# Turning x by block transposes and memory-to-memory copies instead of matrix-engine transposes, and dealing the freed PSUM banks anew

## The chip, the cores and the metric

The kernel runs on one core of a Trainium2 chip. The metric is the device time of one execution in microseconds (us). The kernel before takes 598.78 us, the median of three runs (597.99 to 598.87). Five engines work side by side, each strictly in the order of its own program: PE (matrix products, with its weight loads listed as PEld), DVE (vector), ACT (scalar functions), POOL (a second, slower vector engine) and SP, which here only issues transfers. An engine waits for another one through semaphores. Matrix products land in PSUM, a small memory of banks; everything else lies in the on-chip memory.

## The reference

Eight batches of 576 tokens. Attention with two kinds of narrow masks gives x (576 x 512 per batch), and a token and channel mixer follows:

```python
scores = scale * np.matmul(q, k.transpose(0, 1, 3, 2))
# masks: heads 0-3 a window of 32, heads 4-7 a window of 32 with dilation 4
attn = softmax(np.where(masks, scores, -1e9));  x = np.matmul(attn, v)   # heads side by side
theta = x @ w_theta
zr, zi = x * np.cos(theta), x * np.sin(theta)
y = w_tok_r @ zr + w_tok_i @ zi            # over tokens, per batch
u = x + y
out = u + np.maximum(u @ w_ch, 0.0)
```

So x is needed in two layouts. The attention leaves it with the 128 channels of a pair of heads on the partitions and tokens along the rows (call it x turned), and the products x cos(theta), x sin(theta) need tokens on the partitions.

## The kernel before

All large products are made in float32 quality from split operands: a value is a high part and a low part, and each product is three matmuls (high x high, high x low, low x high). The high part is a cast on ACT, the low part a subtraction on POOL.

One batch goes through these stages. **Scores** (`scores`, L438): for each of four pairs of heads PE makes the scores `s`, DVE adds the mask and takes the row maximum (nine mask instructions, L406), ACT takes nine exponentials (L501), DVE the sums and their reciprocals (L504, L505), POOL scales the rows (L507). **Turn** (`turn`, L511): DVE turns the probabilities by eight block transposes (L522) per pair. **pv** (L600): PE multiplies with v into bank `v`; ACT copies the result out as x turned (`x_evac`, L578), and `x_split` (L582) makes its high and low part. **theta** (L669): five blocks of tokens in the order STS = 4, 0, 1, 2, 3, block 4 being the last 64 tokens; twelve matmuls per full block (L682). **trig** (L722) of a block: ACT rounds theta/2pi to a whole number K (L746), DVE takes the remainder (L748), which frees the bank of theta, ACT takes the sine (L754) and, in `cosine` (L693), the absolute value and the cosine (L695, L697). `natural` (L713) has PE transpose x into a PSUM bank `xn` (four transposes per block, L718), and DVE multiplies `xn` by sine and cosine (L760 and L702; L767 for block 4). `zsplit` (L630) splits each product into the buffers `zh` and `zl` (ACT L641, POOL L643). Block st gives the buffers number st (cosine) and 4 + st (sine); block 4 gives number 8.

**Token units** (`token`, L790): eight units of 27 matmuls (L804) per batch, each over all nine z buffers in the order KORD = 0, 4, 1, 5, 2, 6, 3, 7, 8; DVE then adds the result to x (L782), ACT and POOL split that again (L785, L787). **Channel units** (`chan`, L821): eight units of twelve matmuls (L834) and one DVE instruction each (L813); they share two PSUM banks `m` with the token units.

`phase` (L841) sets the order for batch b and the next batch nb: the eight token units of b with the scores, turns and pv of nb between them, then five times theta, a channel unit and trig, then the three channel units left, and then the next phase begins with the scores of pair 2 and the first token unit. The opening (batch 0 and half of batch 1) is ordered by a planner with ranks (`Order`), since the weights arrive then. Above that, the framework that builds the program runs its own timed model of all engines and moves an instruction of DVE, ACT, POOL or SP when the model says that its input is late; only PE's instructions, and in the opening all that `pin` marks, keep the written order. The sine and the exponential need different tables in ACT; `table` keeps those instructions in written order, so all sines of a phase come before the exponentials of the next.

PSUM before: scores and theta share the two banks `s` with theta's own `t`; `xn` takes `x` and, in turn, the pv bank `v`.

## Time and profile before

| | |
|---|---|
| median of three runs | 598.78 us |
| the profiled execution's own time | 597.07 us |
| its span (first to last instruction) | 595.3 us |
| PE busy | 569.7 us, 96% |
| DVE, ACT, POOL busy | 361.6, 351.1, 222.4 us |
| transposes of x on PE (L718) | 160, 20 per batch |
| one batch in the middle | 211.01 to 279.69 us |

The span lies inside the execution's own time; 1.8 us are outside it. A batch is best read at three points: the end of the last token unit (251.06 us in the batch above), the end of the last channel unit (279.69 us), and the end of the first token unit after it (284.67 us). PE works through one list without a choice, so what it waits for at these points is what a batch costs.

### The profile page before, as it was taken

The page shows a single profiled execution, that of the slowest core. Times are in us where ns is not written, and L with a number is a line of the kernel's source. Part 1 is how long each engine was busy: PE and PEld are TensorE (multiplying, and loading weights), DVE is VectorE, ACT ScalarE, POOL GpSimd, SP SyncE. Part 2 cuts the span into 40 slices and gives each one's busy share as a digit, 9 for nine tenths or more (in the row PEclk, how much of TensorE's full clock was granted, in tenths as well). Part 3 has the DMA queues.
Part 4 walks back from the last instruction along what each step waited for, and adds up shares of the span by engine and source line. Part 5 has one row for each costly group of instructions (what it writes and reads, how often), then busy time and mean ns, then how long its engine had stood idle before and what let it go on. Part 6 is the DMA issues. An engine that isn't in the chain of part 4 may idle for free.

```text
span 595.3 us, 14176 instructions
## 1 busy us (share of the span) xinstructions
PE 569.7 (96%) x5584; PEld 516.9 (87%) x5584; DVE 361.6 (61%) x1132; ACT 351.1 (59%) x939; POOL 222.4 (37%) x206
## 2 busy tenths in 40 slices
PE   5997898999999999999999999999999999999997
PEld 4744787979998899889998899989998899989997
DVE  3889888855765667465566567655665656445112
ACT  1498967687535955568553974468564785266110
POOL 2229854534322532326142442316324253315220
PEclk9999599999999999999999999999999999999999
DMA  8982347404650074302641054401742023001002
GB/s 303 398 339 61 121 160 246 142 1 141 182 160 3 2 241 142 101 2 89 197 139 62 1 181 151 154 1 40 231 142 73 0 81 100 1 1 53 28 1 81
DMA packets 26866, 67.76 MB, mean 114 GB/s; under 512 B 2992, under 2 KB 3248, under 8 KB 26800
## 3 DMA queue, kind: packets, MB, share of 16 engines
q1 hardware_dynamic: 26800, 66.86, 32.9%
q8 instruction: 44, 0.72, 0.5%
q14 instruction: 22, 0.18, 0.1%
HBM read 57.41 MB, written 9.44 MB: 112 GB/s over the span
## 4 chain that ended last, share of the span: by engine, by line
PE 49%; DVE 22%; ACT 21%; issue 3%; POOL 2%; DMA 2%; SPq 0%; ACTq 0%; DVEq 0%; POOLq 0%
PE y L804 27%; DVE pt L522 9%; PE c L834 8%; PE s L465 5%; ACT P L501 5%; PE o L614 4%; PE th L682 3%; ACT K L697 3%; ACT zh L641 3%; ACT g L754 2%; ACT K L695 2%; DVE P L406 2%; DVE K L702 2%; POOL P L507 2%; ACT L754 1%
## 5 line engine op out<-in xcount | busy, mean ns | idle before, releaser
L787 POOL TENSOR_TENSOR u<-x,u 128x288 fp32r<-128x288 f32 x64 | 54.9, 858 | 184.9 <-ACT u L785 162.2
L522 DVE STREAM_TRANSPOSE pt<-P 32x288 f32<-32x288 f32 x224 | 105.1, 469 | 21.1 <-POOL P L507 18.0
L834 PE MATMUL c<-u,late_wc 128*128 128x288 f32 x768 | 111.7, 296 | 0.8 <-DVE x L813 0.5
L834 PEld LDWEIGHTS c<-u,late_wc 128*128 128x128 f32 x768 | 106.2, 188 | 4.8 <-DVE x L813 2.0
L785 ACT CAST u<-x 128x288 fp32r<-128x288 f32 x64 | 27.5, 430 | 129.3 <-DVE x L782 129.3
L804 PE MATMUL y<-wtkh,zh 128*128 128x288 f32 x288 | 90.6, 315 | 1.1 <-ACT zh L641 1.1
L804 PE MATMUL y<-wtkh,zl 128*128 128x288 f32 x288 | 86.6, 301 | 3.7 <-POOL zl L643 3.7
L804 PE MATMUL y<-wtkl,zh 128*128 128x288 f32 x288 | 86.2, 299 | 0.0
L643 POOL TENSOR_TENSOR zl<-g,zh 128x512 fp32r<-128x512 f32 x40 | 52.6, 1316 | 79.1 <-ACT zh L641 66.7
L501 ACT ACTIVATE P<-P,mx 128x64 f32<-128x64 f32 x216 | 72.1, 336 | 16.8 <-DVE mx L495 16.8
L682 PE MATMUL th<-wthh,xh 128*128 128x512 f32 x224 | 76.3, 402 | 0.0
L782 DVE TENSOR_TENSOR x<-y,x 128x288 f32<-128x288 f32 x64 | 28.7, 450 | 66.8 <-PE y L804 64.0
L804 PE MATMUL y<-late_wt_b,zh 128*128 128x288 f32 x320 | 68.1, 297 | 0.0
L804 PE MATMUL y<-late_wt_a,zh 128*128 128x288 f32 x256 | 58.0, 308 | 2.7 <-DVE x L782 2.7
L804 PEld LDWEIGHTS y<-wtkh,zh 128*128 128x128 f32 x288 | 55.4, 192 | 4.8 <-ACT zh L641 2.3
L804 PEld LDWEIGHTS y<-wtkh,zl 128*128 128x128 f32 x288 | 55.3, 192 | 4.5 <-POOL zl L643 4.5
L804 PEld LDWEIGHTS y<-wtkl,zh 128*128 128x128 f32 x288 | 55.5, 193 | 0.3 <-issue 0.3
L643 POOL TENSOR_TENSOR zl<-K,zh 128x512 fp32r<-128x512 f32 x32 | 42.0, 1312 | 36.1 <-ACT zh L641 36.1
L507 POOL TENSOR_TENSOR P<-P,sm 128x576 f32<-128x576 f32 x32 | 37.5, 1172 | 43.8 <-ACT xh L590 19.3
L804 PEld LDWEIGHTS y<-late_wt_b,zh 128*128 128x128 f32 x320 | 51.4, 189 | 0.3
L682 PEld LDWEIGHTS th<-wthh,xh 128*128 128x128 f32 x224 | 42.1, 188 | 8.3
L804 PE MATMUL y<-late_wt_b,zl 128*128 128x288 f32 x160 | 47.3, 296 | 0.0
(103 smaller groups left out, 1110.0 us busy)
## 6 DMA issues: line engine op xcount, KB each, us to landing
q<-in_qT_dram SPq DMA_DIRECT2D x32, 576.0 KB, 4.2
va<-in_vw_dram SPq DMA_DIRECT2D x30, 320.0 KB, 3.2
out_dram<-x SPq DMA_DIRECT2D x32, 288.0 KB, 2.1
k<-in_kT_dram SPq DMA_DIRECT2D x28, 304.0 KB, 4.6
vb<-in_vw_dram SPq DMA_DIRECT2D x29, 256.0 KB, 3.4
st_wtk<-in_wtk_dram SPq DMA_DIRECT2D x8, 576.0 KB, 8.8
st_wth<-in_wth_dram SPq DMA_DIRECT2D x4, 512.0 KB, 9.8
st_wch<-in_wch_dram SPq DMA_DIRECT2D x4, 512.0 KB, 4.9
```

Source lines behind the costliest of these rows:

```text
L465: pe(nc.tensor.matmul(ps[64 * e:64 * e + 64, n - g0], q[:, qb], k[:, QB * qb:QB * qb + BW], start=not masked, stop=not masked or n == g1 - 1))
L501: table(nc.scalar.activation(P[:, n], P[:, n], AF.Exp, bias=mx[:, n:n + 1], scale=SCALE, accum_out=sm[:, n:n + 1]))
L507: pin(nc.gpsimd.tensor_tensor(P, P, sm.unsqueeze(2).to_broadcast([128, NJ, BW]), op=ALU.mult))
L522: pin(nc.vector.transpose(pmats[b, pr][k0:k0 + QB, :, hh, QB * e:QB * e + QB], P[p0:p0 + QB, :, QB * o:QB * o + QB]))
L614: pe(nc.tensor.matmul(ps[64 * hh:64 * hh + 64, BW * j:BW * j + BW], v[:, 64 * hh:64 * hh + 64], pmats[b, pr][:, j, hh], start=True, stop=T ...
L643: pin(nc.gpsimd.tensor_tensor(lo, z, hi.bitcast(F32), op=ALU.subtract))
L682: pe(nc.tensor.matmul(pt, l, r, start=(n == 0), stop=(n == 3 * NC - 1)))
L782: pin(nc.vector.tensor_tensor(x[:, ts], ps, x[:, ts], op=ALU.add))
L785: pin(nc.scalar.copy(uh[b, d][:, ts], x[:, ts]))
L787: pin(nc.gpsimd.tensor_tensor(ul[b, d][:, ts], x[:, ts], uh[b, d][:, ts].bitcast(F32), op=ALU.subtract))
L804: pe(nc.tensor.matmul(ps, l[:, cs], r, start=(n == 0), stop=(n == 3 * NK - 1)))
L834: pe(nc.tensor.matmul(ps, l[:, cs], r[:, ts], start=(n == 0), stop=(n == 3 * NC - 1)))
```

## The change

From batch 1 on PE no longer transposes x. `x_turn` has DVE transpose x turned in blocks of 32 x 32 into a buffer `xq`, one instruction of 128 x 576 per pair of heads. That puts each block right inside itself but leaves the blocks in the wrong place, and `x_move` puts them in place by copies within the on-chip memory: per block of 128 tokens 16 copies of 32 partitions x 128 values (16 KB), 8 for block 4, 72 per batch, all issued by SP. Their target `xn` is not a new buffer but the memory of the z buffers `zh4` to `zh8`, which hold the sine products of the previous batch until its last token unit has read them, and which take this batch's sine products afterwards. So the copies wait for the token units, and the split of the sine product now waits until both products of the block are made. DVE's products read `xn` from the on-chip memory (in a pattern of 16 runs of 32) instead of from PSUM. The theta blocks take the banks `t` and `x` in turn and leave the two banks `s` to the scores; `v` belongs to pv alone. The last hunk makes a descriptor scratch buffer smaller, which this kernel's transfers do not use.

```diff
-TP = {4: "t", 0: "s", 1: "s", 2: "t", 3: "s"}
-XP = {4: "x", 0: "v", 1: "x", 2: "v", 3: "x"}
+TP = {4: "t", 0: "x", 1: "t", 2: "x", 3: "t"}
...
             go(x_split(b, pr))
+            go(x_turn(b, pr))
...
-        pt, rel = yield from bank("t" if b == 1 else TP[st], f"th{b}_{st}")
+        pt, rel = yield from bank(TP[st], f"th{b}_{st}")
...
         yield None, ("xn", b, st)
-        px, rx = pxs[b, st]
         yield "DVE", dve(DM)
-        pin(nc.vector.tensor_tensor(z, px, f, op=ALU.mult))
+        by_x(b, st, z, f)
         signal(key)
         if kt is not None:
-            yield None, ("px", b, st)
-            give(*rx)
+            if not b:
+                yield None, ("px", b, st)
+                give(*pxs[b, st][1])
             yield from zsplit(b, kt, z, rel)
...
+    def x_turn(b, c):
+        yield None, ("xe", b, c)
+        if c == 0:
+            yield from take("xq", 1, b - 1)
+            xq[b] = cp.tile([128, 18, NC, QB], F32, tag="xq", name=f"xq{b}")
+        elif od.live:
+            yield None, ("got", "xq", b - 1)
+        yield "DVE", 1000
+        pin(nc.vector.transpose(xq[b][:, :, c], xf[b, c].rearrange("p (a s) -> p a s", s=QB)))
+        signal(("xq", b, c))
+
+    def x_move(b):
+        for c in range(NC):
+            yield None, ("xq", b, c)
+        if b == 1:
+            for d in range(NC):
+                yield None, ("tk", 0, d, 1)
+        for st in STS:
+            R = 64 if st == 4 else 128
+            kt = min(4 + st, 8)
+            xn = hp.tile([128, DM], F32R, tag=f"zh{kt}", name=f"xn{b}_{st}").bitcast(F32)
+            yield "DMA", dma(R // 128 * DM)
+            for a in range(R // QB):
+                for g in range(4):
+                    pin(nc.sync.dma_start(xn[QB * a:QB * a + QB, 128 * g:128 * g + 128],
+                                          xq[b][QB * g:QB * g + QB, 4 * st + a].rearrange("p a b -> p (a b)")))
+            xns[b, st] = xn[:R].rearrange("p (g c d) -> p c g d", g=4, c=NC)
+            signal(("xn", b, st))
+        give("xq", b - 1)
+
+    def rows(t):
+        return t.rearrange("p (c g d) -> p c g d", c=NC, g=4)
...
+    def by_x(b, st, z, f):
+        if b:
+            pin(nc.vector.tensor_tensor(rows(z), xns[b, st], rows(f), op=ALU.mult))
+        else:
+            pin(nc.vector.tensor_tensor(z, pxs[b, st][0], f, op=ALU.mult))
...
-            pin(nc.vector.tensor_tensor(g, px, g, op=ALU.mult))
+            by_x(b, st, g, g)
             signal(("px", b, st))
+            if b:
+                yield None, ("cos", b, st)
             yield from zsplit(b, 4 + st, g, rg)
...
         rest = UNITS[n:]
+        go(x_move(nb))
         for i, st in enumerate(STS):
             go(theta(nb, st))
...
+    go(x_move(1), 0)
     go(thetas(1), RANK["theta1"])
```

The order of the instructions that results moves at three places. In the rows below the names carry a block (or pair) and a serial number: `K_2` and `g_2` are the cosine and the sine of block 2, `c_3_1` a channel unit, `P_2` and `sm_2` the probabilities and sums of pair 2 of the next batch. Line numbers are each kernel's own: before L702/L760 are the products with x, L748 the remainder, L813 a channel unit's end, L406/L495 mask and maximum, L782 a token unit's end; in the changed kernel these are L764, L794, L860, L405/L494 and L829.

DVE before, at the end of a phase (blocks 1 to 3 of theta, the last channel units, then the next phase's masks):

```order
L702 TENSOR_TENSOR K_1_3365<-xn_1_3360,K_1_3365 128x512
L760 TENSOR_TENSOR g_1_3366<-xn_1_3360,g_1_3366 128x512
L748 SCALAR_TENSOR_TENSOR K_2_3414<-th_2_3382,K_2_3414 128x512
L813 SCALAR_TENSOR_TENSOR x_3_2173<-c_3_0_3395,x_3_2173 128x288
L702 TENSOR_TENSOR K_2_3414<-xn_2_3409,K_2_3414 128x512
L760 TENSOR_TENSOR g_2_3415<-xn_2_3409,g_2_3415 128x512
L748 SCALAR_TENSOR_TENSOR K_3_3464<-th_3_3431,K_3_3464 128x512
L813 SCALAR_TENSOR_TENSOR x_1_1963<-c_1_1_3481,x_1_1963 128x288
L702 TENSOR_TENSOR K_3_3464<-xn_3_3459,K_3_3464 128x512
L760 TENSOR_TENSOR g_3_3465<-xn_3_3459,g_3_3465 128x512
L813 SCALAR_TENSOR_TENSOR x_3_2173<-c_3_1_3511,x_3_2173 128x288
L406 ISA P_2_3526,mx_2_3527<-s_2_0_3529,mskb 128x64
```

DVE at the same place in the changed kernel:

```order
L860 SCALAR_TENSOR_TENSOR x_3_2234<-c_3_1_3682,x_3_2234 128x288
L764 TENSOR_TENSOR K_1_3546<-xn_1_3378,K_1_3546 128x512
L764 TENSOR_TENSOR g_1_3547<-xn_1_3378,g_1_3547 128x512
L405 ISA P_2_3697,mx_2_3698<-s_2_0_3700,mskb 128x64
...
L494 TENSOR_SCALAR mx_2_3698<-mx_2_3698 128x9
L794 SCALAR_TENSOR_TENSOR K_3_3635<-th_3_3607,K_3_3635 128x512
L503 TENSOR_SCALAR sm_2_3699<-sm_2_3699 128x9
L504 RECIPROCAL sm_2_3699<-sm_2_3699 128x9
L764 TENSOR_TENSOR K_2_3590<-xn_2_3395,K_2_3590 128x512
L764 TENSOR_TENSOR g_2_3591<-xn_2_3395,g_2_3591 128x512
L764 TENSOR_TENSOR K_3_3635<-xn_3_3412,K_3_3635 128x512
L764 TENSOR_TENSOR g_3_3636<-xn_3_3412,g_3_3636 128x512
```

Before, the products of blocks 1 to 3 stand among the channel units' ends and all of them ahead of the next masks. Now those of block 1 stand behind the last channel unit, block 3's remainder behind the masks, and the products of blocks 2 and 3 behind the sums of the exponentials of the next phase's first scores. This holds at the end of the phases that lead to batches 2 to 6. At the one that leads to batch 7, where no scores follow, the products of block 1 also stand behind the last channel unit, and block 3's remainder and the products of blocks 2 and 3 follow them at once.

POOL at the same place, before (L643 is the low part of a z buffer, L507 the scaling of `P_2`, L787 the low part of a token unit's sum):

```order
L643 TENSOR_TENSOR zl_5_3379<-g_1_3366,zh_5_3378 128x512
L643 TENSOR_TENSOR zl_2_3423<-K_2_3414,zh_2_3422 128x512
L643 TENSOR_TENSOR zl_6_3428<-g_2_3415,zh_6_3427 128x512
L643 TENSOR_TENSOR zl_3_3473<-K_3_3464,zh_3_3472 128x512
L643 TENSOR_TENSOR zl_7_3478<-g_3_3465,zh_7_3477 128x512
L787 TENSOR_TENSOR u_0_3603<-x_0_2726,u_0_3603 128x288
L507 TENSOR_TENSOR P_2_3526<-P_2_3526,sm_2_3528 128x576
```

and in the changed kernel (the scaling is L506):

```order
L643 TENSOR_TENSOR zl_5_3560<-g_1_3547,zh_5_3559 128x512
L506 TENSOR_TENSOR P_2_3697<-P_2_3697,sm_2_3699 128x576
L643 TENSOR_TENSOR zl_2_3599<-K_2_3590,zh_2_3598 128x512
L643 TENSOR_TENSOR zl_6_3604<-g_2_3591,zh_6_3603 128x512
L643 TENSOR_TENSOR zl_3_3644<-K_3_3635,zh_3_3643 128x512
L643 TENSOR_TENSOR zl_7_3649<-g_3_3636,zh_7_3648 128x512
L834 TENSOR_TENSOR u_0_3774<-x_0_2840,u_0_3774 128x288
```

The scaling of `P_2` has moved ahead of four low parts. ACT has the nine exponentials of `P_2` ahead of the casts zh_2, zh_6, zh_3 and zh_7 in the same way.

SP in the changed kernel, where the copies begin, with what each waits for (`DMAHW0` to `DMAHW7` are eight completion counters that the transfers take in turn):

```order
L219 DMA k_3_3274<-in_kT_dram 128x608
L742 DMA xn_0_3361<-xq_2869 32x128 [waits DVE_49,DMAHW6_49,PE_49,Pool_49]
L742 DMA xn_0_3361<-xq_2869 32x128
L742 DMA xn_0_3361<-xq_2869 32x128 [waits DMAHW0_49]
L742 DMA xn_0_3361<-xq_2869 32x128 [waits DMAHW1_49]
L742 DMA xn_4_3352<-xq_2869 32x128 [waits DMAHW2_49,PE_49]
L742 DMA xn_4_3352<-xq_2869 32x128 [waits DMAHW3_49]
```

All 72 copies stand between the last loads of k and v for a phase and the four stores of the batch's result. Each waits until the transfer eight places ahead of it has landed.

15 lines of the change are left out of this document (9 added, 6 removed).

## The prediction

> **What bounds the kernel now.** I read the page's first lines, then busy time by windows, then the chain of waits.
>
> ```profile
> span 595.3 us, 14176 instructions
> PE 569.7 (96%) x5584; PEld 516.9 (87%) x5584; DVE 361.6 (61%) x1132; ACT 351.1 (59%) x939; POOL 222.4 (37%) x206
> ```
>
> PE is the only engine near its limit; an average, so I look at one batch. The windows are 211.01 (scores of pair 2 begin) to 251.06 (last token unit ends), to 279.69 (last channel unit ends), to 284.71 (first token unit of the next phase ends); columns are PE, PEld, DVE, ACT, POOL busy, then clock and transfers.
>
> ```profile
> 211.01:251.06 40.05, 39.52 (x506) 37.85 (x506) 25.29 (x120) 21.19 (x83) 12.46 (x13) 1.00 0.51 166
> 251.06:279.69 28.63, 28.35 (x176) 25.20 (x176) 17.41 (x34) 21.01 (x39) 11.88 (x11) 1.00 0.06 21
> 279.69:284.71 5.02, 5.02 (x67) 4.79 (x67) 2.02 (x21) 4.13 (x18) 2.24 (x2) 1.00 0.84 285
> ```
>
> PE idles 0.8 us in 68.68: 211.01 to 279.69 is one batch, and each of the three stretches is as long as PE's work in it. The chain of waits shows the same, piece by piece:
>
> ```profile
> 276.23 3.46 PE c L834 x24
> 279.69 1.20 PE s L465 x36
> 280.89 3.78 PE y L804 x27
> ```
>
> The first token unit needs all nine z buffers and starts 1.2 us after the channel units. Before, it never waits for them. I call the ends of the last token unit, of the channel units and of the first token unit U, T and E: T - U = 28.63, E - T = 4.98, and E to the next U 35.1 us.
>
> **What leaves PE.** Twenty transposes per batch, in five groups. The timeline of PE (start, duration, engine, line) at block 4 of theta, a channel unit, a full block, another channel unit and a group:
>
> ```profile
> 251.06 0.39 PE L687 MATMUL th<-wthh,xh 128*128 128x512 f32 x1
> ...
> 252.90 1.74 PE L834 MATMUL c<-u,late_wc 128*128 128x288 f32 x12
> ...
> 254.84 0.48 PE L682 MATMUL th<-wthh,xh 128*128 128x512 f32 x1
> ...
> 257.66 1.74 PE L834 MATMUL c<-u,late_wc 128*128 128x288 f32 x12
> 259.24 0.60 PE L718 MATMUL xn<-idt,x 128*128 128x128 f32 x4
> 259.59 0.47 PE L682 MATMUL th<-wthh,xh 128*128 128x512 f32 x1
> ```
>
> A group holds PE 0.35 us from start to start (259.24 to 259.59), five groups 1.75. Block 4 of theta takes 1.84 (251.06 to 252.90), a full block 2.82 (254.84 to 257.66), a channel unit 1.58 (257.66 to 259.24): 1.84 + 4 x 2.82 + 8 x 1.58 = 25.8, which leaves 2.8 of T - U for the groups and about 1 us of waits for channel banks, which go too, since DVE's channel ends no longer stand behind products. I take -2.7 per batch, bounds -1.75 and -2.9. If nothing else happened, six batches like that and one in the opening would give -18.
>
> **What becomes late.** The diff does not show it, the order does: on DVE the products of blocks 2 and 3 now follow the sums of the next phase's exponentials. DVE works in order, so I walk from T along the engines with these durations (timelines of DVE, ACT and POOL at the end of this batch, and of ACT and DVE around the exponentials after the previous one):
>
> ```profile
> 278.60 0.68 DVE L760 TENSOR_TENSOR g<-xn,g 128x512 f32<-128x512 f32 x1
> 279.19 1.00 DVE L813 SCALAR_TENSOR_TENSOR x<-c,x 128x288 f32<-128x288 f32 x2
> 281.90 0.17 DVE L495 TENSOR_SCALAR mx<-mx 128x9 f32<-128x9 f32 x1
> 273.80 0.58 ACT L746 ACTIVATE K<-th 128x512 int32<-128x512 f32 x1
> 275.13 0.68 DVE L748 SCALAR_TENSOR_TENSOR K<-th,K 128x512 f32<-128x512 f32 x1
> 275.91 0.63 ACT L754 ACTIVATE g<-K 128x512 f32<-128x512 f32 x1
> 277.23 0.72 ACT L697 ACTIVATE K<-K,halfpi 128x512 f32<-128x512 f32 x1
> 278.71 0.62 ACT L641 CAST zh<-K 128x512 fp32r<-128x512 f32 x1 [0.76 <-DVE K L702]
> 279.95 1.28 ACT L501 ACT_TABLE_LOAD   x1
> 213.42 0.35 ACT L501 ACTIVATE P<-P,mx 128x64 f32<-128x64 f32 x1 [0.86 <-DVE mx L495]
> 216.56 0.18 DVE L504 TENSOR_SCALAR sm<-sm 128x9 f32<-128x9 f32 x1
> 216.77 0.22 DVE L505 RECIPROCAL sm<-sm 128x9 f32<-128x9 f32 x1
> 279.41 1.27 POOL L643 TENSOR_TENSOR zl<-K,zh 128x512 fp32r<-128x512 f32 x1 [1.52 <-ACT zh L641]
> 280.65 1.28 POOL L643 TENSOR_TENSOR zl<-g,zh 128x512 fp32r<-128x512 f32 x1
> ```
>
> The last channel end leaves DVE at T + 0.5 (279.19 + 1.00). Two products of 0.6 (from one start to the next, 278.60 to 279.19): T + 1.8. The first one's cast on ACT: T + 1.85; its low part on POOL, 1.28: T + 3.2. Only that frees the buffer in which ACT writes block 3's K (two such buffers go round): T + 3.8, the remainder on DVE 0.68: T + 4.55; the nine masks, which before were done by T + 2.2 (281.90), have ended by T + 3.5 behind the two products. Sine, absolute value, cosine on ACT run 2.05 us (275.91 to 277.95): T + 6.6. The table of the exponential 1.28: T + 7.9. Nine exponentials 3.1 (213.42 to 216.53): T + 11.05. Sum and reciprocal: T + 11.5. Now the four products, 2.4: the first at T + 12.2, the last at T + 14.0. POOL scales P_2 first (1.2 us as in the fence below, to T + 12.7) and then makes four low parts, one per 1.26: T + 17.9. PE needs the last of them for one matmul and then has three more of 0.13 (27 in 3.78 are 0.14 each): E = T + 18.4. Against T + 4.98 that is **+13.4** per batch. It replaces the slack that the products had among the channel units; what is late next is everything behind E, since PE has no other work there: the order has the token unit next. This walk without any further delay is the bound from below.
>
> **Products from memory beside POOL.** They read both inputs from memory now. Nearest row, the low part of x, also 128x512 from two inputs in memory:
>
> ```profile
> L596 DVE TENSOR_TENSOR xh<-x,xh x21: 677/686/1646, 101.1 to 509.8; 128x512 fp32r<-128x512 f32 x21
> 229.16 1.21 POOL L507 TENSOR_TENSOR P<-P,sm 128x576 f32<-128x576 f32 x1 [3.21 <-ACT xh L590]
> 229.28 1.65 DVE L596 TENSOR_TENSOR xh<-x,xh 128x512 fp32r<-128x512 f32 x1
> ```
>
> Alone it takes 0.686, as from PSUM. When POOL had started 0.12 us earlier, it ended at 230.93, 0.56 after POOL's end: it stood still until then. From T + 11.5 on POOL is never idle, so between 0 and 2.4 us (four products beside five POOL instructions, all in line) is added. I take **+1.9**, near the row in which both ran.
>
> The Trainium skill, "SBUF — State Buffer", section "Who interferes with whom", states that a DVE instruction with two on-chip inputs and a GpSimd instruction that reads the same memory exclude each other for their whole length. The trace agrees in the pair of rows above. By that rule the term would be the full 2.4 and the time some 3 us longer; by the median row it would be 0 and the time 10 us shorter.
>
> **The clock of PE.** PE waits for long only in the opening, and there a steady run of matmuls follows from 66.5 on:
>
> ```profile
> 66.00:71.00 5.00, 4.48 (x18) 4.48 (x19) 2.80 (x8) 5.00 (x27) 4.37 (x5) 0.50 0.01 3
> 71.00:76.00 5.00, 5.00 (x41) 4.92 (x41) 4.83 (x10) 4.86 (x9) 5.00 (x4) 0.96 0.00 0
> ```
>
> For about 4.7 us after work is steady again the granted clock stays at 0.50; of such 4.7 us about half is lost. I take **+2.1** behind each E and +0.4 for the last matmuls before it; bounds 0 and 3.
>
> **DVE's block transposes.** Four per batch, 128x576. Nearest row:
>
> ```profile
> L522 DVE STREAM_TRANSPOSE pt<-P 32x288 f32<-32x288 f32 x224 | 105.1, 469 | 21.1 <-POOL P L507 18.0
> ```
>
> If the time goes by elements in a row, 576 is 2 x 0.469 = 0.94; if by all elements, 8 x 0.469 = 3.75. A product of 128 partitions takes 0.68 / 512 = 1.3 ns per element of a row, this transpose of 32 partitions 0.469 / 288 = 1.6: the number of partitions hardly counts in these rows, so I take 0.9. They stand in front of the low parts of x and of the turns of P, where DVE is busy 25.29 of 40.05 us; a walk of that stretch like the one above finds one place that pinches, the end of the third token unit on DVE, at E + 17.6 behind a turn, whose bank PE wants at E + 17.2; in exchange the 0.5 us wait of that kind before the last unit goes. That is 0. At 3.75 each (15 per batch) DVE has 41 us for a 35 us stretch: +6 per batch.
>
> **The copies.** 72 per batch, on a queue where each waits for the one eight ahead.
>
> ```profile
> idb<-in_identb_dram SPq DMA_DIRECT2D x1, 32.0 KB, 1.7
> 237.69 0.33 SPq L231 DMA_DIRECT2D va<-in_vw_dram  x1
> ```
>
> Landing in 1.7 allows one per 0.21; issuing costs 0.33 for a load of 128 partitions. I take 0.3 each: they begin when zh4 has been read, U - 2.7, and the last lands near U + 21, before T. Needed are 24 at U + 15, 40 at T + 0.5, 56 at T + 11.5, 72 at T + 12.7 (T = U + 25.9). So they are hidden by the chain above; on their own they decide from 0.55 us per copy on. SP's queue behind them holds the result's stores, which wait for T + 0.5 anyway, and the loads of the next pair, used after E + 16: covered. That a product waits for eight counters instead of one I count as nothing beside these terms.
>
> **The banks.** theta block 1 takes the bank that block 4's remainder frees.
>
> ```profile
> 259.64 0.68 DVE L748 SCALAR_TENSOR_TENSOR K<-g,K 64x512 f32<-64x512 f32 x1 [0.33 <-ACT K L746]
> ```
>
> Before, that remainder ended at U + 9.3; block 1 could now start at U + 7.8 (1.84 + 1.58 + 2.82 + 1.58). Were DVE not earlier, PE would wait 1.5. But the turn of P_1 ahead of it on DVE waits for exponentials that hang on masks, and in my walk these come about 1 to 2 us earlier after E than before, since DVE has nothing else left to do there. I take 0, bounds 0 and +1.5.
>
> **Sum.** Per transition into batches 2 to 6: -2.7 + 13.4 + 1.9 + 0.4 + 2.1 = +15.1, times five = **+75.5**. Into batch 7 no scores follow, so the walk skips table, exponentials and P_2: K_3's remainder at T + 4.55, its cosine at T + 6.6, its products at T + 7.9, low parts to T + 12.4 (four from T + 7.3), E = T + 12.95. Before, from the chain of waits:
>
> ```profile
> 550.34 28.62 PE y L804 x216
> ```
>
> There (T = 550.34) E = T + 3.6 (an eighth of 28.62): +9.3, with 0.5 for POOL, 2.5 for the clock and -1.9 for PE's transposes **+10.4**. In the opening (batch 1; first row from the chain, second from DVE's timeline):
>
> ```profile
> 118.88 0.69 DVE g L743
> 141.26 0.69 DVE L702 TENSOR_TENSOR K<-xn,K 128x512 f32<-128x512 f32 x1
> ```
>
> The last block transpose stands just ahead of block 4's first instruction on DVE (118.88 before), so the copies start near 120 and end, at 0.3 each, near 144; the last product with x began at 141.26, so its low parts come some 5 us later while PE gains 1.8: **+4**, bounds -2 and +6. Together +90 on the profiled execution's 597.07: 687. The median is 1.7 above the profiled execution, so **688**.
>
> Its own range: with contention, clock and opening at their lower bounds (+10.7 x 5 + 7 - 2 = +59) 657; at the upper ones (block 1's bank, 2.4 and 3 for every batch, opening +6) about +110, 708.
>
> **Rivals.** (1) *PE's relief is all that counts*, the products come when PE wants them: 598.8 - 18 = 581. For it: PE at 96%. Against it: the order of DVE and ACT, which nothing at run time changes. 3%. (2) *The copies set the pace*: at 0.7 us each the last lands at U + 50, 11 later than the chain needs it, 67 more in six batches: 755. For it: many small copies in one queue; against it: 1.7 us for 32 KB with eight under way. 7%. (3) *The block transposes cost by all elements*: 6 x 6 more, 725. 8%. (4) *PE has room in the wait*, as if DVE's blocks overlapped better than my walk, half of the 13.4: 640 to 655. 5%. That x is still turned on PE is excluded by the order. My forecast has the remaining 77%.
>
> A measurement of this kernel tells 0.2% (1.2 us) from no change. Faster 3%, the same 1%, slower 96%. The range of 650 to 730 leaves out rivals 1 and 2, the lower part of 4 and the outer ends of 3.
>
> **What would show it.** Right: PE idle some 12 us behind T in batches 2 to 6, ended by zl (POOL) and zh (ACT); scaling of P_2 ahead of four low parts; PE's clock near 0.5 behind it; a batch of about 84 us; products of 0.69 alone and up to 1.9 beside POOL; copies landed before T. Wrong: DVE's products waiting on `xn` copies (rival 2), block transposes far above 1 us (rival 3), or a first token unit that ends before T + 15.

## The result and the profile after

The changed kernel takes 746.87 us, the median of four runs (744.9 to 747.51), against 598.83 us (597.99 to 598.95) for the kernel before: a ratio of 1.247, 95% interval 1.244 to 1.250. The prediction had the sign and missed the size: +148 where +90 was expected, and 746.9 lies outside the range of 650 to 730. The profiled execution took 744.9 us of which the span is 743.0.

The first lines of the page and its chain of waits by line (what each line of the program holds of the way to the end):

```profile
span 743.0 us, 14681 instructions
PE 591.1 (80%) x5444; PEld 522.6 (70%) x5444; DVE 388.4 (52%) x1160; ACT 352.9 (48%) x939; POOL 222.6 (30%) x206
PEclk9998999869999689995999859996799958997599
SPq L742 37%; PE y L851 17%; DVE pt L521 7%; ACT P L500 4%; PE o L613 3%; PE c L881 3%; POOL zl L643 2%; PE s L464 2%; DMA xn<-xq 2%; DVE P L405 1%; DVE xq L725 1%; DVE xh L595 1%; ACT x L577 1%; POOL P L506 1%; ACT zh L641 1%
```

Before, the chain was PE from one batch to the next. Now 37% of it, some 275 us, is SP issuing the copies (L742), and once per batch PE's clock drops. The copies seen by their tile, with the shortest, median and longest duration in ns, and from the same answer what the idle time in front of the instructions that write or read `xn` ended with (us, times) and how long a copy takes from its issue until its data has landed:

```profile
L742 SPq DMA_DIRECT2D xn<-xq x504: 507/589/1484, 119.0 to 693.0; - x168
  DMA xn<-xq: 74.1, 17
DMA to landing us min/median/max: 1.7/1.8/3.6
```

DVE's products waited 74 us for copies. A copy holds SP 0.589 us in the median, where the prediction took 0.3. SP's timeline in one middle batch gives the pace:

```profile
299.65 44.81 SPq L742 DMA_DIRECT2D xn<-xq  x68
```

68 of the batch's 72 copies in 44.81 us are 0.66 us each, one right behind the other. With 1.8 us to land, some three are under way at once (an estimate, 1.8 / 0.66), so that a copy has to wait for the one eight places ahead is not what sets this pace. The windows of that batch, with the points of the prediction, are E to U, U to T, T to E:

```profile
262.40:299.75 37.35, 36.71 (x443) 35.09 (x443) 25.77 (x102) 17.03 (x64) 8.55 (x10) 0.95 0.45 145
299.75:325.63 25.88, 25.88 (x155) 22.90 (x154) 13.30 (x27) 14.90 (x29) 6.52 (x6) 1.00 0.12 26
325.63:351.30 25.67, 9.29 (x65) 6.55 (x65) 7.76 (x29) 10.57 (x29) 9.61 (x7) 0.61 0.31 98
```

The batch takes 88.9 us, 20.2 more than before. T - U is 25.88, as PE's work without the transposes was worked out (25.8 to 25.9). From U to T, with copies issued all the time, the transfer engines are busy 12% of the time (the last figure but one of that row): it is not they that are short. T to E is 25.67 instead of 4.98; the prediction had 20.7. What DVE did there:

```profile
325.67 0.46 DVE L860 SCALAR_TENSOR_TENSOR x<-c,x 128x288 f32<-128x288 f32 x1 [1.14 <-PE c L881]
336.88 0.21 DVE L504 RECIPROCAL sm<-sm 128x9 f32<-128x9 f32 x1
337.25 0.69 DVE L764 TENSOR_TENSOR K<-xn,K 128x512 f32<-128x512 f32 x1 [0.16 <-DMA xn<-xq]
337.86 1.64 DVE L764 TENSOR_TENSOR g<-xn,g 128x512 f32<-128x512 f32 x1
345.98 0.69 DVE L764 TENSOR_TENSOR K<-xn,K 128x512 f32<-128x512 f32 x1 [6.47 <-DMA xn<-xq]
```

Up to the reciprocal the walk of the prediction is met: it ends at 337.09, T + 11.5. Block 2's products then find their copies just landed. Block 3's first product stands until 345.98, T + 20.35, for the last sixteen copies.

To see where the 148 us went I cut the span of both profiles at the end of the last token unit of batch 1 and of batch 6, which leaves the opening, five equal periods and the rest. Before, then after:

```profile
0.00:182.50 182.50, 164.33 (x1793) 137.63 (x1794) 133.09 (x369) 121.41 (x330) 82.32 (x73) 0.95 0.53 184
182.50:522.60 340.10, 336.28 (x3310) 312.91 (x3309) 206.73 (x722) 206.25 (x571) 121.39 (x115) 1.00 0.29 93
522.60:595.30 72.70, 69.07 (x484) 66.32 (x482) 21.75 (x41) 23.45 (x40) 18.71 (x18) 0.99 0.09 33
```

```profile
0.00:211.80 211.80, 164.07 (x1773) 136.81 (x1774) 140.16 (x377) 121.21 (x330) 80.87 (x73) 0.92 0.48 164
211.80:649.90 438.10, 354.01 (x3209) 318.22 (x3208) 226.45 (x742) 207.81 (x571) 123.14 (x115) 0.88 0.28 86
649.90:743.00 93.10, 73.05 (x464) 67.53 (x462) 21.82 (x41) 23.92 (x40) 18.58 (x18) 0.87 0.12 38
```

| | before | after | difference | predicted |
|---|---|---|---|---|
| opening, to the end of batch 1's token units | 182.5 | 211.8 | +29.3 | +4 |
| five periods | 340.1 | 438.1 | +98.0 | +75.5 |
| the rest (into batch 7) | 72.7 | 93.1 | +20.4 | +10.4 |
| sum | 595.3 | 743.0 | +147.7 | +90 |

All three parts are short, the opening most. Rows of DVE's timeline there, and one of the chain of waits (PE's last channel units):

```profile
135.65 0.69 DVE L764 TENSOR_TENSOR g<-xn,g 128x512 f32<-128x512 f32 x1 [9.44 <-DMA xn<-xq]
156.65 0.69 DVE L764 TENSOR_TENSOR g<-xn,g 128x512 f32<-128x512 f32 x1 [9.44 <-DMA xn<-xq]
157.86 0.45 DVE L860 SCALAR_TENSOR_TENSOR x<-c,x 128x288 f32<-128x288 f32 x1
```

```profile
158.37 7.49 PE c L881 x36
```

In the opening the channel units' ends are pinned on DVE behind products. They waited with them for copies, PE waited for the banks that these ends free, and its last three channel units ran only from 158.37 on; they took 7.49 us, where three such units are 4.7 at the 1.58 of the prediction.

### The profile page after: what moved, and what is told of

Same layout as the page of the kernel before. It is cut to its first block, busy times and chain, and to the rows that moved or that the text cites. A ratio compares the mean times of both kernels' runs of the same rounds, so it can differ in the third digit from the quotient of the medians.

```text
span 743.0 us, 14681 instructions
## 1 busy us (share of the span) xinstructions
PE 591.1 (80%) x5444; PEld 522.6 (70%) x5444; DVE 388.4 (52%) x1160; ACT 352.9 (48%) x939; POOL 222.6 (30%) x206
## 4 chain that ended last, share of the span: by engine, by line
SPq 37%; PE 25%; DVE 16%; ACT 8%; issue 6%; POOL 3%; DMA 3%; DVEq 0%; ACTq 0%; POOLq 0%
SPq L742 37%; PE y L851 17%; DVE pt L521 7%; ACT P L500 4%; PE o L613 3%; PE c L881 3%; POOL zl L643 2%; PE s L464 2%; DMA xn<-xq 2%; DVE P L405 1%; DVE xq L725 1%; DVE xh L595 1%; ACT x L577 1%; POOL P L506 1%; ACT zh L641 1%
## 5 line engine op out<-in xcount | busy, mean ns | idle before, releaser
L851 PE MATMUL y<-wtkh,zh 128*128 128x288 f32 x288 | 97.5, 339 | 79.7 <-ACT zh L641 79.7
L881 PE MATMUL c<-u,late_wc 128*128 128x288 f32 x768 | 110.9, 300 | 14.0 <-DVE x L860 11.9
L851 PEld LDWEIGHTS y<-wtkh,zh 128*128 128x128 f32 x288 | 59.6, 207 | 87.0 <-ACT zh L641 84.6
L881 PEld LDWEIGHTS c<-u,late_wc 128*128 128x128 f32 x768 | 108.6, 193 | 17.4 <-DVE x L860 12.1
L851 PE MATMUL y<-wtkh,zl 128*128 128x288 f32 x288 | 96.6, 335 | 24.7 <-POOL zl L643 23.0
L834 POOL TENSOR_TENSOR u<-x,u 128x288 fp32r<-128x288 f32 x64 | 51.8, 809 | 204.0 <-ACT u L832 200.5
L851 PE MATMUL y<-wtkl,zh 128*128 128x288 f32 x288 | 90.6, 314 | 0.0
L851 PEld LDWEIGHTS y<-wtkh,zl 128*128 128x128 f32 x288 | 58.8, 204 | 36.7 <-POOL zl L643 36.7
L643 POOL TENSOR_TENSOR zl<-g,zh 128x512 fp32r<-128x512 f32 x40 | 52.1, 1305 | 107.5 <-ACT zh L641 94.7
L643 POOL TENSOR_TENSOR zl<-K,zh 128x512 fp32r<-128x512 f32 x32 | 43.7, 1367 | 103.9 <-ACT zh L641 103.9
L506 POOL TENSOR_TENSOR P<-P,sm 128x576 f32<-128x576 f32 x32 | 39.8, 1245 | 72.1 <-DVE sm L504 65.7
L851 PEld LDWEIGHTS y<-wtkl,zh 128*128 128x128 f32 x288 | 60.0, 208 | 0.3 <-issue 0.3
L829 DVE TENSOR_TENSOR x<-y,x 128x288 f32<-128x288 f32 x64 | 28.7, 449 | 56.9 <-PE y L851 56.3
L641 ACT CAST zh<-K 128x512 fp32r<-128x512 f32 x32 | 19.7, 616 | 75.2 <-DVE K L764 75.1
```

Source lines behind the costliest of these rows:

```text
L506: pin(nc.gpsimd.tensor_tensor(P, P, sm.unsqueeze(2).to_broadcast([128, NJ, BW]), op=ALU.mult))
L641: pin(nc.scalar.copy(hi, z))
L643: pin(nc.gpsimd.tensor_tensor(lo, z, hi.bitcast(F32), op=ALU.subtract))
L829: pin(nc.vector.tensor_tensor(x[:, ts], ps, x[:, ts], op=ALU.add))
L834: pin(nc.gpsimd.tensor_tensor(ul[b, d][:, ts], x[:, ts], uh[b, d][:, ts].bitcast(F32), op=ALU.subtract))
L851: pe(nc.tensor.matmul(ps, l[:, cs], r, start=(n == 0), stop=(n == 3 * NK - 1)))
```

## The experiments

Two readings stood against each other. **A**: the number of copies times what SP needs to issue one sets the pace. **B**: the bytes, or the transfers' own time, set it. A third, **C**, is the prediction's own main term: the late place of the products on DVE costs about 13 us per batch by itself. All times below are medians; the ratio to the kernel before comes with its 95% interval.

### Half the copies, twice the size

```diff
-                for g in range(4):
-                    pin(nc.sync.dma_start(xn[QB * a:QB * a + QB, 128 * g:128 * g + 128],
-                                          xq[b][QB * g:QB * g + QB, 4 * st + a].rearrange("p a b -> p (a b)")))
+                for g in (0, 2):
+                    pin(nc.sync.dma_start(xn[QB * a:QB * a + QB, 128 * g:128 * g + 256],
+                                          xq[b][QB * g:QB * g + QB, 4 * st + a - a % 2:4 * st + a - a % 2 + 2].rearrange("p n a b -> p (n a b)")))
```

> The changed kernel with 36 copies per batch in place of 72, each of 32 partitions x 256 values in place of 128: the same bytes, half the instructions. Two neighbouring 32-token blocks travel together, so x arrives in the wrong place and the products are of wrong values; every engine's work keeps its size. With fewer copies the framework puts the products back among the channel units, as before the change. Theory A (what a copy costs SP's queue to issue, about 0.65 us whatever it carries, sets the pace): 36 x 0.65 = 23 us, the last copy lands about 22 us after the last token unit, before its product wants it near 24; PE's relief is what is left: 598.8 - 18 + 4 in the opening = 585, range 575 to 605. Theory B (the bytes, or the transfers' own time, set the pace): a copy costs 1.3 us, the last lands as late as in the changed kernel, 735 to 750. Theory C (the late products cost their 13 us per transition by themselves): as that order is gone here, C expects what A expects; the run with the late order held tells them apart.

606.58 us, ratio 1.014 (1.011 to 1.018): 140 us of the 148 are gone with the same bytes moved. SP's timeline in a middle batch, PE's channel units with the idle time ahead of them, one of PE's waits among the token units (PE's timeline), and the opening as a window:

```profile
331.57 23.71 SPq L742 DMA_DIRECT2D xn<-xq  x36
```

```profile
L881 PE MATMUL c<-u,late_wc 128*128 128x288 f32 x768 | 111.0, 298 | 14.6 <-DVE x L860 12.2 <-DVE x L829 2.4
```

```profile
330.57 0.53 PE L851 MATMUL y<-late_wt_a,zh 128*128 128x288 f32 x2 [1.08 <-DVE x L829]
```

```profile
0.00:196.80 196.80, 165.90 (x1773) 138.91 (x1774) 139.11 (x377) 121.98 (x335) 80.94 (x73) 0.95 0.51 177
```

A copy of 32 KB takes SP 0.66 us, exactly what one of 16 KB took. B falls. The order also changed, as expected of the framework: without any other edit, its model put the products back among the channel units. So the late order is not an independent cause: with half the copies it is gone, and the framework moves an instruction when its model has the input late. A's number, 585 in a range that ended at 605, was too good: PE now waits for the banks of channel and token units, and the opening still loses 14 us (196.8 against 182.5).

### The late order held by hand, with half and with all copies

From batch 2 on the generators that make a block's products stop at a mark and are resumed later: block 1's after the last channel unit, those of blocks 2 and 3 after the next phase's first scores, each resumed product tied to the DVE instruction ahead of it.

```diff
-        yield "DVE", dve(DM)
+        yield "HOLD" if b > 1 and st in (1, 2, 3) else ("DVE", dve(DM))
         by_x(b, st, z, f)
...
+            release(4)
             f, i, g = UNITS[n]
             go(f(b, i, g))
...
-            go(trig(nb, st))
+            if st != 3:
+                go(trig(nb, st))
...
             f, i, g = rest.pop(0)
             go(f(b, i, g))
+        release(2)
+        go(trig(nb, 3))
```

> The same 36 double copies (values wrong in the same way), but the changed kernel's order held by hand from batch 2 on: block 1's products behind the last channel unit, the products of blocks 2 and 3 behind the sums of the next phase's first exponentials. This is the prediction's walk without the slow copies. If the walk was right: first token unit ends 18.4 to 20.7 us after the channel units, period 82 to 84 us, whole kernel 687, range 670 to 705. If the copies were all that mattered and the order is harmless: 580 to 605. If bytes set the pace (theory B): 735 to 750.

> A control for the run with 36 copies and the late order: the same order held by hand with all 72 copies; the result is the reference's. It should behave as the changed kernel, 747, range 740 to 755; were it much slower or faster, the hand-held order would not stand for the changed kernel's.

The control with all copies gives 745.13 us (1.247, 1.243 to 1.251), the changed kernel's time. With 36 copies the same order gives 696.88 us (1.165, 1.162 to 1.169), near the 687 of the walk. Cut at the same two points:

```profile
0.00:195.70 195.70, 166.68 (x1773) 139.34 (x1774) 139.19 (x377) 122.08 (x335) 80.99 (x73) 0.94 0.51 178
195.70:614.00 418.30, 351.73 (x3209) 317.47 (x3208) 240.31 (x742) 206.90 (x566) 127.60 (x115) 0.90 0.29 90
614.00:696.00 82.00, 72.63 (x465) 67.27 (x463) 22.54 (x41) 23.30 (x40) 18.66 (x18) 0.94 0.13 43
```

The five periods are 78.2 us above the kernel before (predicted 75.5) and the rest 9.3 (predicted 10.4). Only the opening, +13.2 for +4, is off. The end of a phase in this run, DVE then POOL:

```profile
305.51 0.46 DVE L862 SCALAR_TENSOR_TENSOR x<-c,x 128x288 f32<-128x288 f32 x1 [1.14 <-PE c L883]
317.10 0.69 DVE L764 TENSOR_TENSOR K<-xn,K 128x512 f32<-128x512 f32 x1 [0.16 <-issue]
317.71 1.64 DVE L764 TENSOR_TENSOR g<-xn,g 128x512 f32<-128x512 f32 x1
319.28 1.75 DVE L764 TENSOR_TENSOR K<-xn,K 128x512 f32<-128x512 f32 x1
320.95 1.76 DVE L764 TENSOR_TENSOR g<-xn,g 128x512 f32<-128x512 f32 x1
```

```profile
317.12 1.69 POOL L506 TENSOR_TENSOR P<-P,sm 128x576 f32<-128x576 f32 x1 [7.29 <-DVE sm L504]
318.77 1.71 POOL L643 TENSOR_TENSOR zl<-K,zh 128x512 fp32r<-128x512 f32 x1
323.80 1.27 POOL L643 TENSOR_TENSOR zl<-g,zh 128x512 fp32r<-128x512 f32 x1
```

T is 305.5, the first product starts at T + 11.6 (predicted to end at T + 12.2), the last low part ends at T + 19.6, the first token unit at 326.45, T + 20.95 (predicted 20.7). The two engines take turns: each DVE product ends about 0.55 us after the POOL instruction that it met, and POOL's next then needs 1.71 in place of 1.27. The Trainium skill, "SBUF — State Buffer", section "Who interferes with whom", states that a DVE instruction with two inputs in the on-chip memory and a GpSimd (POOL) instruction that reads that memory exclude each other; the rows agree, in both directions.

So C is right about the order's price and wrong about the whole: on top of it the slow copies cost 745.1 - 696.9 = 48 us.

### The early order, with all copies

```diff
-            pin(nc.vector.tensor_tensor(rows(z), xns[b, st], rows(f), op=ALU.mult))
+            tc.keep_in_program_order(nc.vector.tensor_tensor(rows(z), xns[b, st], rows(f), op=ALU.mult))
```

The same replacement is made for the channel ends, the remainder and the masks.

> The changed kernel with all 72 copies, but DVE's order near that of the kernel before: remainder and products of a block right behind the channel unit's end that follows it, all ahead of the next masks; the result is the reference's. Theory A (the copies' issue sets the pace): the last copy lands 45 to 46 us after the last token unit as before; on DVE the channel units' ends now stand behind waiting products, so PE does its last channel units after the last copy, as in the opening of the changed kernel, where three of them took 7.5 us: some 5 us more per transition, 747 + 6 x 5 = 777, range 755 to 800. Theory C (the order is what costs): back to 600 to 620.

765.4 us (1.280, 1.277 to 1.283), inside A's range and slower than the changed kernel. Idle time of DVE ahead of the instructions on `xn`:

```profile
  DMA xn<-xq: 176.0, 27
```

It waits 176 us instead of 74. PE's longest sum of waits in this run (us, times, longest one) is for the ends of channel units; in the changed kernel that row has 11.9:

```profile
PE c L881 <- DVE x L860: 117.8, 19, 12.0
```

Putting the order right without making the copies cheaper makes the kernel slower, since channel units then wait as well. The four cells:

| | late order | early order |
|---|---|---|
| 72 copies | 746.9 (held by hand 745.1) | 765.4 |
| 36 copies | 696.9 | 606.6 |

### Two issuing engines

```diff
-                    pin(nc.sync.dma_start(xn[QB * a:QB * a + QB, 128 * g:128 * g + 128],
+                    pin((nc.sync if g % 2 else nc.scalar).dma_start(xn[QB * a:QB * a + QB, 128 * g:128 * g + 128],
```

> The changed kernel with every second copy issued by ACT in place of SP, 36 each; the result is the reference's. In ACT's order its copies all stand ahead of the next batch's trigonometry. Theory A (each copy costs its own issuing engine 0.65 us): SP is done 23 us after its first copy, and so is ACT, whose 21 us of work between the last token unit and the first of the next phase then start about 20 us late: first token unit ends near U + 45 against U + 51.6 in the changed kernel and U + 30.9 before, so 700, range 670 to 725. Theory B (the transfers themselves, on the shared transfer engines, set the pace): 72 copies still take 47 us, ACT is held until U + 44, 830 or more. The Trainium skill, page on DMA engines, states that issuing from several engines only saves the issuing engines' time, which it calls usually small; by that the pace would not change.

732.72 us (1.225, 1.223 to 1.228): above A's range, far below B's. The timelines of SP and ACT in one batch:

```profile
381.07 24.05 SPq L742 DMA_DIRECT2D xn<-xq  x36
```

```profile
385.58 21.18 ACTq L742 DMA_DIRECT2D xn<-xq  x33
406.80 0.58 ACT L787 COPY g<-th 64x512 f32<-64x512 f32 x1 [20.85 <-DMA xn<-xq]
```

Both issue side by side at 0.64 to 0.67 us per copy, so the cost belongs to the issuing engine and not to the transfers. ACT does nothing else meanwhile and starts the trigonometry at 406.8, 22.9 us after the last token unit (383.9). From there the first token unit took 28 us; I had taken ACT's 21 us of busy time, without its waits for DVE, and that is where A's number went wrong. The Trainium skill, "DMA: Bandwidth & Descriptors", section "Issuing engines are not separate DMA queues", says that a second issuing engine saves only the issuing engine's time, which it calls usually small against the transfer. The first half agrees: the landing time stayed 1.8 us, and what was saved is issue. The second does not fit here: 0.6 us of issue is a third of the landing, and as landings overlap and issues on one engine do not, the issue is the whole pace.

### Wide copies, and no copies

```diff
-            for a in range(R // QB):
-                for g in range(4):
-                    pin(nc.sync.dma_start(xn[QB * a:QB * a + QB, 128 * g:128 * g + 128],
-                                          xq[b][QB * g:QB * g + QB, 4 * st + a].rearrange("p a b -> p (a b)")))
+            for g in range(4):
+                pin(nc.sync.dma_start(xn[:R, 128 * g:128 * g + 128],
+                                      xq[b][:R, 14 + g if st == 4 else 4 * st + g].rearrange("p a b -> p (a b)")))
```

> The changed kernel with 20 copies per batch of 128 partitions x 128 values (64 partitions for block 4): the same bytes, a quarter of the instructions, x in the wrong place. It measures what a copy within the on-chip memory costs SP when it spans 128 partitions. Prediction's step: 0.33 us, the duration of a load of 128 partitions; if instead a copy costs what it cost at 32 partitions, 0.59 to 0.65. In both cases 20 copies are hidden, order as with 36 copies, 600 to 606. If the bytes set the pace: 735 or more.

603.79 us (1.010, 1.008 to 1.012). The copies by their tile:

```profile
L741 SPq DMA_DIRECT2D xn<-xq x140: 471/599/1578, 119.3 to 541.3; - x140
```

A copy over 128 partitions costs SP 0.599 us in the median, one over 32 partitions 0.589. The number of partitions is not what makes a copy dear; the load of 128 partitions at 0.33 that the prediction leaned on was another kind of transfer. A small part of the difference is the place in line. The first copy of the batch above, in the changed kernel, found SP free:

```profile
296.90 0.52 SPq L742 DMA_DIRECT2D xn<-xq  x1
```

It took 0.52 us where those behind it take 0.59. The 0.19 us between 0.52 and the 0.33 of a load remain; no run shows why.

```diff
-            xn = hp.tile([128, DM], F32R, tag=f"zh{kt}", name=f"xn{b}_{st}").bitcast(F32)
-            yield "DMA", dma(R // 128 * DM)
-            for a in range(R // QB):
...
+            xn = xq[b][:, 4 * st:4 * st + 4].rearrange("p n c s -> p (n c s)") if R == 128 else xq[b][:, 14:18].rearrange("p n c s -> p (n c s)")
```

> The changed kernel without any copy: the products read the block-transposed x where it lies, in the same access pattern, so the values are wrong and only the transfer of x is left out; block transposes, banks and PE's relief stay. This bounds from below what the rest of the change does. Theory A: what the 36-copy run still has above PE's relief is not the copies but PE's waits for channel banks behind DVE's products (1.6 us per batch) and the opening, 606 with 8 us of it the opening's copies: 598, range 590 to 605. If the block transposes or the reads from on-chip memory cost what rival 3 of the prediction said: above 620.

604.06 us (1.011, 1.009 to 1.013; its seven runs spread from 600.1 to 606.5, and the profiled one is the lowest, 4 us under the median). Cut as before:

```profile
0.00:188.70 188.70, 161.76 (x1773) 134.51 (x1774) 140.47 (x377) 121.28 (x330) 81.19 (x73) 0.95 0.51 178
188.70:527.80 339.10, 326.68 (x3209) 302.44 (x3208) 239.10 (x742) 202.99 (x571) 128.26 (x115) 1.00 0.29 94
527.80:598.40 70.60, 66.95 (x464) 64.13 (x462) 24.42 (x41) 23.12 (x40) 18.81 (x18) 1.00 0.09 34
```

Even with x free of charge the change is no gain. PE is busy 9.6 us less in the five periods (326.7 for 336.3), and the periods are 1.0 us shorter. Its freed time became waits, most of them for the banks of token and channel units, whose ends stand on DVE behind block transposes and products. And the opening stays 6.2 us behind with no copy in it; which of the planner's shifts there does this was not tried.

### The opening alone

Batch 1 is treated as before (PE transposes, bank `x`); the rest is the changed kernel.

```diff
-            go(x_turn(b, pr))
+            if b > 1:
+                go(x_turn(b, pr))
...
-        if b:
+        if b > 1:
             return
-        px, rx = yield from bank("mmxxm"[st], f"xn{b}_{st}")
+        px, rx = yield from bank("mmxxm"[st] if b == 0 else "x", f"xn{b}_{st}")
...
-    go(x_move(1), 0)
```

> The changed kernel with batch 1 handled as before the change (PE transposes its x into the bank x, theta in bank t), copies from batch 2 on; the result is the reference's. The changed kernel reaches the end of batch 0's channel units at 165.9 us against 142.4 before. If that whole loss is due to batch 1's copies, it goes: 747 - 23 = 723, range 717 to 729. If it comes from the planner's other shifts: 740 or more.

717.29 us (1.199, 1.196 to 1.202), 29.6 less than the changed kernel:

```profile
0.00:181.90 181.90, 157.27 (x1793) 131.39 (x1794) 136.87 (x373) 121.87 (x330) 82.27 (x73) 0.99 0.53 185
```

The opening is back at 181.9 (182.5 before). All of its +29.3 came with batch 1's part of the change: about 16 of it from the copies' pace (211.8 against 195.7 with half the copies), 7 from the 36 copies that are left there (188.7 without any), 6 without any copy.

### By way of DRAM

Nine large transfers per batch in place of 72 small ones.

```diff
+        xd = dp.tile([S, DM], F32, tag="xd", name=f"xd{b}")
+        go_back = xd.rearrange("(n q) (g e) -> g q n e", q=QB, g=4)
+        for g in range(4):
+            yield "DMA", dma(18 * 32)
+            pin(nc.sync.dma_start(go_back[g], xq[b][QB * g:QB * g + QB].rearrange("p n c s -> p n (c s)")))
...
-            for a in range(R // QB):
-                for g in range(4):
-                    pin(nc.sync.dma_start(xn[QB * a:QB * a + QB, 128 * g:128 * g + 128],
-                                          xq[b][QB * g:QB * g + QB, 4 * st + a].rearrange("p a b -> p (a b)")))
+            pin(nc.sync.dma_start(xn[:R], xd[128 * st:128 * st + R]))
```

> The changed kernel with the 72 copies replaced by nine large transfers per batch, the result still the reference's: after the block transposes four stores (32 partitions x 18 runs of 512 B each) put x in token order into a scratch tensor in DRAM, and five loads of whole token blocks bring it to the same xn buffers, issued by SP as the copies were. Theory A (the number of issues on SP's queue sets the pace): nine issues of 0.3 to 0.6 us, 3 to 5 us per batch; the stores run before the z buffers come free, the loads land within some 5 us of that, the framework puts the products back among the channel units, and the time is that of the run with 36 copies or a little below: 606, range 595 to 612. Theory B (x's way through the transfer engines is what takes long, whatever the number of issues): the same 1.2 MB must now go twice, 747 or more.

> The run by way of DRAM with, in addition, batch 1 handled as before the change (PE transposes its x); the result is the reference's. With the whole loss of the opening gone (there the run by way of DRAM is some 10 us behind the kernel before) and the middle batches within 0.4 us of those before: 598, range 592 to 603. If the middle batches carry the loss: 606 or more.

610.18 us (1.020, 1.019 to 1.022) for the first, 597.46 (0.9996, 0.9985 to 1.0007) with batch 1 as before. The transfers by their tile in the first:

```profile
L746 SPq DMA_DIRECT2D xn<-xd x35: 326/382/1220, 127.0 to 537.5; - x35
L737 SPq DMA_DIRECT2D xd<-xq x28: 325/844/1630, 119.2 to 529.9; - x28
```

The same bytes travel twice, and 137 us are gone: by the medians five issues of 0.38 us and four of 0.84 (these between 0.33 and 1.63) instead of 72 of 0.59. This is the plainest case against B.

### A third bank for the units

Both runs go by way of DRAM with batch 1 as before. The first gives bank `x` to the pool `m` from the start; the second, whose edit is shown, lends it to the units from batch 2 on.

```diff
-TP = {4: "t", 0: "x", 1: "t", 2: "x", 3: "t"}
+TP = {4: "t", 0: "s", 1: "s", 2: "t", 3: "s"}
...
-        ps, rel = yield from bank("m", f"c{b}_{e}_{g}")
+        ps, rel = yield from bank(unit(b), f"c{b}_{e}_{g}")
...
+    def unit(b):
+        units_made.append(b)
+        return "x" if b > 1 and len(units_made) % 3 == 0 else "m"
```

> The same with the banks dealt otherwise: the bank x that the PE transposes leave becomes a third bank for the token and channel units (bank m), and theta keeps the banks it had before the change (t and, shared with the scores, s). In the runs with cheap copies PE waits 1.4 us per batch for a channel bank and 1 us for a token bank, both behind DVE's queue. If these waits are what eats PE's relief, they go: 2.4 us in each of six batches less than the run with two such banks, 584, range 578 to 592, faster than the kernel before. If PE then waits for theta's bank s instead, as much as it gained: 598, no change.

> The run by way of DRAM with batch 1 as before the change, and bank x as a third bank for token and channel units from batch 2 on only, so that the opening keeps its two banks; the result is the reference's. In the run that had three banks throughout, the opening lost 8 us against the kernel before (end of batch 0's channel units 150.6 against 142.4) and the rest gained 5.3 (from there to the last channel unit 444.0 against 449.3). With the opening of the run with two banks (143.9) and that rest: 143.9 + 444.0 = 587.9 against 591.7, so 598 - 4 = 594, range 590 to 598. If the third bank only moves the wait to the end of the trigonometry of block 3 (ACT, DVE, POOL one after the other), the gain stays below 2 us: 596 to 598.

With three banks from the start: 599.56 us (1.003, 1.002 to 1.004), the expectation of 584 missed: up to the last channel unit of batch 0 it lost 8.2 us against the kernel before (150.6 against 142.4), and from there to the last channel unit it gained 5.3 (444.0 against 449.3). With the third bank from batch 2 on only: 594.55 us against 597.90, ratio 0.995 (0.993 to 0.997), faster than both kernels by a little. The five periods and the waits of PE's channel units in that run:

```profile
184.00:522.10 338.10, 325.31 (x3209) 302.27 (x3208) 227.26 (x742) 203.01 (x571) 126.19 (x115) 1.00 0.43 131
L891 PE MATMUL c<-u,late_wc 128*128 128x288 f32 x768 | 110.2, 296 | 9.2 <-DVE x L870 9.2
```

PE's work fell by 11 us in the five periods (325.3 for 336.3) and the time by 2. PE still waits 9 us for channel ends on DVE, even with three banks: they stand in DVE's queue behind products that wait for sine and cosine. So the next limit seems to be the trigonometry behind the last theta block; that is read from the waits, no run tested it.

## Why the prediction was wrong, by its steps

**The copies, 0.3 us each.** This is the step that failed. A copy holds SP 0.589 us and the pace is 0.65 to 0.66. The prediction named the point from which they decide, 0.55, and gave the case beyond it, rival 2, 7% at 0.7 us and 755. The mechanism is rival 2's. That the time is only 8 us from its figure is in part luck: rival 2 put 11 us into each of six transitions, 67 in all, and none into the opening. By the runs the copies' pace, with the late order held, costs 745.1 - 696.9 = 48 us; between the spans of the changed kernel and of the run with half the copies it is 47: 20 in the five periods, 11 into batch 7, 16 in the opening. Of the 58 us that the prediction was short, these 47 are the copies, 9 the rest of the opening, 3 the five periods, and -1 the way into batch 7.

The size rested on the issue of a load from DRAM, 0.33, rounded down, as if any issue cost this. No row before showed a copy within the on-chip memory, and the upper bound that such a gap calls for was left out of the range. The trace before had one more sign: a load of k is issued right behind one of q and holds SP longer.

```profile
L218 SPq DMA_DIRECT2D q<-in_qT_dram x28: 327/328/1025, 24.4 to 449.4; - x28
L220 SPq DMA_DIRECT2D k<-in_kT_dram x28: 328/426/1280, 25.4 to 449.7; - x28
```

Even its 0.43 would have stayed under 0.55, so what no row could give is what a copy costs over a load.

**A sign that was there.** The prediction took the late order as given and asked what it costs. Half the copies alone gave the early order back, so the framework's model had counted 72 of them as too slow for the early one. At 0.3 each the prediction had all of them landed before T, in time for the early order; the late order did not fit that. The model's figures are not on record, so this is a sign and no measurement.

**The walk from T, +13.4, and POOL, +1.9.** Right: with the copies out of the way the first token unit ends at T + 20.95 (20.7 predicted), reciprocal and first product are within 0.1 us, five periods +78.2 (75.5). POOL's last low part ends at T + 19.6, 1.7 behind the 17.9 of the walk without contention (+1.9 taken). In the changed kernel itself the last 4.7 of T + 25.7 come from the copies.

**Clock, +2.1 behind E.** Right: E to U is 37.35 at a mean clock of 0.95, against 35.1.

**PE's 20 transposes, -2.7.** Right where the order is late (T - U 25.88 for 28.63). With the early order the relief turns into waits for banks, and five periods are 1.0 us shorter instead of 13.5. Rival 1's 581 was out of reach by another road than the one it was dismissed for.

**Block transposes.** 0.72 to 0.78 us each for the 0.9 taken; rival 3 falls. Its price was read wrongly too: DVE's 25.29 us and 15 more are 40.3, and the window that they were read from is 40.05 us long, not 35.

**Banks and the place that pinches, 0.** Right in the changed kernel, where PE works without a gap from U to T and waits 0.2 us in E to U for a token unit's bank. In the early order with half the copies it did pinch: PE waits 1.08 us for such a bank.

**The opening, +4.** Wrong by 25. Of the +29.3, 23 are the same copies, through channel units pinned on DVE behind the products that wait for them, and 6 no copy explains. The prediction looked at the last product there and not at what stands behind it on DVE.

**Into batch 7, +10.4.** +20.4 in the changed kernel, +9.3 with half the copies: the copies again.

**The last addition.** 687 + 1.7 is 689 and not 688; nothing hangs on it.

## What to carry to other kernels

A transfer has three prices: its bytes, its latency and the time its issuing engine spends on it (here 16 KB, 1.8 us and 0.59 us). With 72 small ones in a row the last one was the pace. So count the transfers, multiply by a measured issue of the same kind, taken from transfers in line, and where there is none let the range hold twice the nearest row, as it was here. Before mending the order that a scheduler made, mend the length that made it choose that order; restoring the order alone was some 19 us slower here.

## What the runs showed of the hardware

- A copy from on-chip memory to on-chip memory cost its issuing engine 0.59 to 0.60 us in the median, the same for 16, 32 and 64 KB, for 32 and 128 partitions, and for SP and ACT (0.593 and 0.601), when copies followed one another; it cost 0.52 us where it was the first in line (32 partitions). A load from DRAM cost 0.33 us alone and 0.43 us right behind another. Why the copy is dearer stays open.
- Two engines issuing such copies at once did not slow each other: 0.67 and 0.64 us each beside 0.66 for one alone, landing 1.8 us as with one.
- DVE and POOL, both reading two on-chip operands, alternate: 1.64 to 1.76 us in place of 0.69 on DVE, 1.7 in place of 1.27 on POOL.
